# Attention, a gated layer and routed experts in one kernel: four routing tables, a moved sum and bound instruction orders

## The chip, the cores and the metric

The kernel is one program on 1 core of a Trainium2 chip. The metric is the device time of one execution in microseconds (us), shown as the median of several runs. Five engines take part: TensorE (PE) for matrix products, VectorE (DVE), ScalarE (ACT), GpSimd (POOL) and SyncE (SP), which here only issues DMAs and reads registers. POOL issues DMAs too, all the indirect ones among them.

## The reference, cut to what matters

```
attn = softmax(mask(q k^T / 8 + bias)) v        # 4 x 8 heads, 576 positions, 64 wide, window of 128
x    = attn as [2304, 512]
x    = (sigmoid(x w_gate) * (x w_val)) w_out    # [512, 1536] twice, [1536, 512]
logits = normalised(x) . normalised(expert_emb) / tau      # 8 experts
e      = argmax(logits)                                     # one expert for each token
out[t] = softmax(logits)[t, e] * (relu(x[t] w1[e]) w2[e])   # [512, 1024], [1024, 512]
```

All of it is in float32. The kernel makes each float32 product from three products of a high and a low part, so most operands are first split: ACT casts the high part and DVE subtracts it to get the low part.

## The kernel before, in words

The 2304 tokens are 18 tiles of 128. They are worked on in chunks of 2, 4, 4, 4 and 4 tiles. The gated layer takes chunks 1 to 4 in two groups of two (`PAIRS`), and each group uses a scheme of seven products in place of eight, for which sums of input halves (S1 to S4, built by `sum_x`) and of weight parts (T1 to T4, `sum_w`) are needed. `seven` lists the seven products m1 to m7 of one block f of 128 columns, with what evicts them: e1 copies bank a into the row c11, f6 into r1, e7 into c22, e4 into c21, and the products in bank a go on accumulating after each copy.

What the layer gives is kept for the product with w_out as sums too (`keep_g`): for two blocks f it forms four sums, S3, S2, S4 and S1, and stores each tile to DRAM. For the first group these sums are put off in a list, from which `catch_up` takes them later. Three of them are left when the second group's loop over f (12 blocks) begins.

Small tiles of [128, 513] come from the pool `mid`, which has ten of them (`row`). Operand tiles of 4 KB a partition come from a pool of 33 (`slot`).

The product with w_out runs over 14 steps (`SEQ`), each with two halves, and then once more for chunk 0 (`mm2`). Between these steps the table `AT2` places the routing of each finished block b of four tiles: `rx` turns its rows and takes their norm, `ra` (`route_a`) makes the logits and writes the rows with their gate weight to `x2_d` in DRAM, `route_b` counts each token's place among those of its expert with small products (`rk`), and scatters the token numbers into tables in DRAM (`tab_d`) with one indirect DMA for each tile. Blocks 3, 7 and 1 come first; then `close` fixes which experts start early and gathers three tiles of their tokens. The blocks of `LATE` are routed afterwards, their tokens placed behind these tiles (`bump`). Rows of x2 that are not yet there when the early gathers run are filled with zeros by `zero_rows`.

`places` reads token numbers from the tables: one DMA for each table and a `min`, since an empty place holds 2304. `gather` reads the rows. `by_count` orders the experts by their counts, and SP then reads that order into registers for the addresses of weight loads. The experts run in that order (`ffn1`, `ffn2`, or `tok_a` and `tok_b` for a single tile), with the weights of the next expert loaded and split meanwhile. At the end a loop over overflow tiles follows; its plan is the list of small DVE instructions from `pn` to `ov`, and its count `nov` is read by every engine.

The attention part and most of the first group are written out in program order. From the last nine products of the first group on, a planner orders each engine's instructions by its own cost estimates, with earlier program order first. `tc.keep_in_program_order(i)` binds an instruction behind the one traced before it on its engine, and `tc.issue_after(i)` binds what follows on that engine behind i; neither waits for i to finish. On each engine the order is then fixed, and an instruction that waits holds up those behind it.

Of the kernel before, what the change touches and what calls it, by code (L numbers as in the profile page):

```python
# [22 lines left out]
NT = B * S  # L23
# [18 lines left out]
LATE = (5, 6, 0)  # L42
# [3 lines left out]
NMID = 10  # L46
NWARM = 7
CHUNKS = [2, 4, 4, 4, 4]
PAIRS = [(2, 1), (4, 3)]
# [9 lines left out]
def attn_ffn_moe(ctx: ExitStack, tc: tile.TileContext, qkd, vd, wgv, w_out, emb, tau, w1, w2, cst, ids, out):  # L59
# [10 lines left out]
    tab_d = [dram.tile([P * E * TCOL, 1], I32, tag=f"tab_d{y}", name=f"tab_d{y}") for y in range(2)]  # L70
# [257 lines left out]
    def sum_x(key, x, y, op, q=nc.vector):  # L328
        t = slot([P, 2, 512], F32, f"xq_{key}")
        q.tensor_tensor(out=t, in0=x, in1=y, op=op)  # L330
        xf[key] = t

    def builds(pair):
        one, two = PAIRS[pair]

        def src(half, k):
# [6 lines left out]
            "S4+": lambda: sum_x((pair, "S4"), src(0, 1), xf[pair, "S2"], ALU.subtract, nc.gpsimd if pair else nc.vector),  # L343
# [102 lines left out]
    def catch_up(n=1):  # L446
        for t in [put_off.pop(0) for _ in range(min(n, len(put_off)))]:
            t()
# [4 lines left out]
    def keep_g(pair, f, half, gate, val, keep_val=True):  # L453
# [6 lines left out]
        def sums(name, t, x, y, op):  # L460
            def form():
                o = t()
                nc.vector.tensor_tensor(out=o, in0=K[x], in1=K[y], op=op)
# [414 lines left out]
    bB["S4+"]()  # L878
    WO_AT = [[], [0], [1], [2], [3], [4], [5, 6], [7], [8], [9], [10], []]
    for f in range(KF):  # L880
# [6 lines left out]
        if f == 0:  # L887
            bB["A22"]()
            bB["S4"]()
# [17 lines left out]
        if f < 3:  # L907
            catch_up()
# [38 lines left out]
    def places(o, x, c0, q):  # L947
        for t, v in zip((o, x), tab_v):
            q.dma_start(t, v[:, bass.ds(c0, o.shape[1])])
        nc.vector.tensor_tensor(out=o, in0=o, in1=x, op=ALU.min)  # L950


    def zero_rows():
        zrow = row("zrow")
        tc.keep_in_program_order(nc.gpsimd.memset(zrow, 0.0))
        nc.gpsimd.dma_start(x2_d[NT:NT + 1, :], zrow[0:1, :])
        for b in LATE:
            for u in range(2):
                nc.gpsimd.dma_start(x2_d[(2 * b + u) * P:(2 * b + u + 1) * P, :], zrow)
# [18 lines left out]
    cp.tile([P, 8], I32, tag="pad", name="pad")  # L978
    idx0, idx1 = (cp.tile([P, 2 * CE], I32, tag=f"idx{y}", name=f"idx{y}") for y in range(2))
    routed, mark, reg = {}, {}, {}  # L980
# [26 lines left out]
    def route_a(b, ss, xr, c=None):  # L1007
# [17 lines left out]
        nc.scalar.copy(parts, part[:, 0:nu * P])  # L1025
        lp = pt("s", f"lp{b}", 2)
# [32 lines left out]
    def route_b(b):  # L1059
# [41 lines left out]
    def by_count(c, less, o, n):  # L1101
# [539 lines left out]
```

## Time and profile before

| what | value |
|---|---|
| median of 3 runs | 819.44 us (818.62 to 820.49) |
| the profiled execution | 817.23 us |
| its span, first to last instruction | 815.6 us |
| mean granted clock of PE | 0.988 of full speed |
| PE busy | 782.7 us, 96% of the span |
| DVE, ACT, POOL busy | 72%, 56%, 27% |
| HBM traffic | 216 GB/s over the span |

The span is that of the profiled execution, and what lies around it is the rest of that execution's own time. PE's busy time counts pipelined products by modelled ends, so that busy isn't the same as at its peak. Where PE idles, the view of waits tells which instruction on which engine ended the idle time. A product of 512 columns starts 0.23 us after the one before it at full clock.

### The profile page before, as it was taken

How to read it: one execution, taken by the hardware profiler on the slowest of the kernel's cores; microseconds unless marked ns; L12 is line 12 of the kernel's file. 1: busy time of each engine (PE TensorE's matmuls, PEld its weight loads, DVE VectorE, ACT ScalarE, POOL GpSimd, SP SyncE). 2: the span in 40 equal slices, each digit the busy share in tenths (PEclk: the TensorE clock that was granted, in tenths of full speed). 3: DMA queues.
4: the chain of work that ended last, by engine and by line, in shares of the span. 5: the costliest groups of instructions: out<-in, count | busy, mean ns of one | idle time of the engine just before them, and what ended most of it. 6: DMA issues, size and time to landing. Idle time of an engine off the chain costs nothing. (4 is left out here: it accounts for less than half of the span.)

```text
span 815.6 us, 15736 instructions
## 1 busy us (share of the span) xinstructions
PE 782.7 (96%) x5585; PEld 654.1 (80%) x5585; DVE 585.7 (72%) x1361; ACT 452.7 (56%) x955; POOL 219.1 (27%) x343
## 2 busy tenths in 40 slices
PE   9989999999999899999999999979899999999996
PEld 6767888878887688887787777757679989899995
DVE  7988978888899978897867587717656564446621
ACT  6888766666545455556656667646345443354510
POOL 6856423322001022232100033534422120402100
PEclk9999999999999899999999999989999999999999
DMA  8686468765674698999875487673459555626100
GB/s 284 185 269 217 157 254 282 269 234 192 230 255 175 212 374 322 342 344 383 338 257 181 156 238 229 132 221 93 152 181 319 182 184 180 204 104 230 58 25 19
DMA packets 73761, 176.64 MB, mean 217 GB/s; under 512 B 10548, under 2 KB 18612, under 8 KB 73680
## 3 DMA queue, kind: packets, MB, share of 16 engines
q1 hardware_dynamic: 63248, 145.07, 51.9%
q0 software_dynamic: 10432, 30.53, 11.3%
q8 instruction: 45, 0.74, 0.4%
q14 instruction: 36, 0.29, 0.1%
HBM read 120.93 MB, written 55.35 MB: 216 GB/s over the span
## 5 line engine op out<-in xcount | busy, mean ns | idle before, releaser
L1175 PE MATMUL h<-xe,weh 128*128 128x256 f32 (+4 forms) x512 | 105.3, 299 | 0.1
L116 POOL TENSOR_SCALAR p<-p,rs 128x192 f32<-128x192 f32 x140 | 77.0, 569 | 91.3 <-DVE rs L267 54.5
L120 DVE TENSOR_TENSOR wel<-wer,weh 128x1024 fp32r<-128x1024 f32 x64 | 76.9, 1220 | 25.3 <-ACT weh L104 9.8
L1175 PEld LDWEIGHTS h<-xe,weh 128*128 128x128 f32 x512 | 83.2, 188 | 1.5 <-DVE h L1178 0.7
L251 ACT ACTIVATE p<-p,mx 128x192 f32<-128x192 f32 x144 | 64.1, 447 | 27.6 <-DVE mx L248 27.3
L1175 PE MATMUL h<-xe,wel 128*128 128x256 f32 (+4 forms) x256 | 76.2, 298 | 0.0
L104 ACT CAST weh<-wer 128x1024 fp32r<-128x1024 f32 x64 | 66.2, 1048 | 15.8 <-DMA wer<-in_w 10.6
L1193 PE MATMUL z<-weh,h 128*128 128x512 f32 (+1 forms) x224 | 72.0, 398 | 0.7 <-ACT h L1177 0.7
L1177 ACT ACTIVATE h<-h 128x256 fp32r<-128x256 f32 (+4 forms) x64 | 26.7, 418 | 76.8 <-PE h L1175 75.3
L1178 DVE SCALAR_TENSOR_TENSOR h<-h,h 128x256 fp32r<-128x256 f32 (+4 forms) x64 | 29.4, 463 | 39.4 <-ACT h L1177 39.0
L120 DVE TENSOR_TENSOR ol<-ol,oh 128x1024 fp32r<-128x1024 f32 x42 | 49.7, 1217 | 9.7 <-ACT oh L104 9.7
L1193 PEld LDWEIGHTS z<-weh,h 128*128 128x128 f32 (+1 forms) x224 | 40.8, 186 | 10.0 <-ACT h L1177 0.9
L1175 PEld LDWEIGHTS h<-xe,wel 128*128 128x128 f32 x256 | 48.3, 188 | 0.0
L1298 PE MATMUL b<-oh,wo 128*128 128x512 f32 x144 | 44.9, 393 | 0.0
L1193 PE MATMUL z<-wel,h 128*128 128x512 f32 (+1 forms) x112 | 44.2, 394 | 0.0
L1198 POOL DMA_INDIRECT out<-y,cols x13 | 14.3, 1101 | 102.3 <-DVE y L1197 97.8
L104 ACT CAST oh<-ol 128x1024 fp32r<-128x1024 f32 x42 | 41.4, 1048 | 0.0
L1197 DVE TENSOR_SCALAR y<-z,xg 128x512 f32<-128x512 f32 (+1 forms) x16 | 12.0, 748 | 37.6 <-PE z L1193 37.6
L1298 PE MATMUL b<-oh,th 128*128 128x512 f32 x96 | 38.1, 401 | 0.0
L1298 PE MATMUL b<-oh,tl 128*128 128x512 f32 x96 | 38.1, 397 | 0.0
L1298 PE MATMUL b<-ol,th 128*128 128x512 f32 x96 | 37.9, 395 | 0.0
L237 PE MATMUL s<-qk 64*64 64x128 f32 (+2 forms) x864 | 34.6, 278 | 1.6 <-DVE mx L248 0.7
(481 smaller groups left out, 2222.7 us busy)
## 6 DMA issues: line engine op xcount, KB each, us to landing
wer<-in_w SPq DMA_DIRECT2D x64, 512.0 KB, 5.2
wr<-in_wgv SPq DMA_DIRECT2D x24, 512.0 KB, 5.9
qk<-in_qkd SPq DMA_DIRECT2D x36, 320.0 KB, 3.9
v<-in_vd SPq DMA_DIRECT2D x36, 192.0 KB, 3.5
wor<-in_w_out SPq DMA_DIRECT2D x12, 512.0 KB, 6.3
ol<-g0S SPq DMA_DIRECT2D x12, 512.0 KB, 6.6
ol<-g1S SPq DMA_DIRECT2D x12, 512.0 KB, 5.0
wq_d<-wh SPq DMA_DIRECT2D x10, 512.0 KB, 2.8
```

Source lines behind the costliest of these rows:

```text
L104: nc.scalar.copy(o, i)
L116: nc.gpsimd.tensor_scalar(out=t, in0=t, scalar1=r, scalar2=0.0, op0=ALU.mult, op1=ALU.add)
L120: e.tensor_tensor(out=o, in0=i, in1=h.bitcast(F32), op=ALU.subtract)
L237: nc.tensor.matmul(ss[u][y * 64:(y + 1) * 64, j * WK + d:j * WK + d + n], q[halves[u], a:a + 64], k[halves[u], a + c0:a + c0 + n], start=T ...
L251: nc.scalar.activation(out=o, in_=o, func=AF.Exp, scale=-1.0, bias=mx[:, z:z + 1], accum_out=su[:, z:z + 1])
L1175: nc.tensor.matmul(m[:, :n], w[:, fs], x[:, k, :], start=(cnt == 0), stop=(cnt == 3 * KD - 1))
L1177: nc.scalar.activation(out=hh, in_=m[:, :n], func=AF.Relu)
L1178: nc.vector.scalar_tensor_tensor(out=hl, in0=m[:, :n], scalar=0.0, in1=hh.bitcast(F32), op0=ALU.max, op1=ALU.subtract)
L1193: nc.tensor.matmul(m[0:w, :], h, ww[:, ds], start=(cnt == 0), stop=(cnt == 3 * KE - 1))
L1197: nc.vector.tensor_scalar_mul(y[0:w, :], m[0:w, :], x[0:w, DM:DM + 1])
L1198: nc.gpsimd.indirect_dma_start(out=out, out_offset=IOA(ap=idx[0:w], axis=0), in_=y[0:w, :], in_offset=None, bounds_check=NT - 1, oob_is_er ...
L1298: nc.tensor.matmul(bk[pair, z], p, q, start=(first and kk == 0 and y == 0), stop=(kk == KF // 2 - 1 and y == 2), skip_group_check=True)
```

## The change

Six edits, most of them about the order of the work.

1. There are four routing tables instead of two, one for each tile of a block. `places` reads all four into one tile and takes the minimum in two steps, so it issues four DMAs where it issued two. The tables are cleared by four DMAs at the start.
2. The halves of the second group are exchanged, (3, 4) for (4, 3), and with them the blocks 5 and 7 in the order of routing. The block routed after `close` is then 7, with the highest token numbers, and the early gathers are bounded to the first 14 tiles. `zero_rows` clears the end row and the first two tiles, where it cleared six tiles, and is placed at step 5 of the second product in place of step 11. The memsets of the tiles for the early gathers are bound behind what was traced before them on POOL, and each expert's gathers follow its table reads.
3. The sum S4 of the second group is formed on DVE in place of POOL, and traced after A22 in block 0.
4. The three sums that are left of the first group are bound to the end of blocks 0, 1 and 2.
5. The register loads of the experts' order are bound behind the SP instructions traced before them, and the overflow plan behind what was traced last on each engine when expert 3 begins.
6. `route_a` can stop before the small product that folds the logits (`route_l`, which waits for `parts`); for blocks 7 and 0 that part comes one place later.

A padding tile grows from 8 to 16 columns, and the tiles `more` of the table reads become two that are used in turn, so that the tiles behind them keep their offsets modulo 128 bytes.

```diff
-LATE = (5, 6, 0)
+LATE = (7, 8, 0)
+NE = (LATE[0] - 1) * 2 + 2
+NTAB = 4
-PAIRS = [(2, 1), (4, 3)]
+PAIRS = [(2, 1), (3, 4)]
...
-            "S4+": lambda: sum_x((pair, "S4"), src(0, 1), xf[pair, "S2"], ALU.subtract, nc.gpsimd if pair else nc.vector),
+            "S4+": lambda: sum_x((pair, "S4"), src(0, 1), xf[pair, "S2"], ALU.subtract),
...
-    def catch_up(n=1):
+    def catch_up(n=1, pin=False):
         for t in [put_off.pop(0) for _ in range(min(n, len(put_off)))]:
-            t()
+            t(pin)
...
-            def form():
+            def form(pin=False):
                 o = t()
-                nc.vector.tensor_tensor(out=o, in0=K[x], in1=K[y], op=op)
+                i = nc.vector.tensor_tensor(out=o, in0=K[x], in1=K[y], op=op)
+                if pin:
+                    tc.keep_in_program_order(i)
...
     bB["S3"]()
-    bB["S4+"]()
...
             bB["A22"]()
+            bB["S4+"]()
             bB["S4"]()
...
         if f < 3:
-            catch_up()
+            catch_up(pin=True)
...
     def places(o, x, c0, q):
-        for t, v in zip((o, x), tab_v):
-            q.dma_start(t, v[:, bass.ds(c0, o.shape[1])])
-        nc.vector.tensor_tensor(out=o, in0=o, in1=x, op=ALU.min)
+        for y, v in enumerate(tab_v):
+            q.dma_start(x[:, y, :], v[:, bass.ds(c0, o.shape[1])])
+        nc.vector.tensor_tensor(out=x[:, 0:2, :], in0=x[:, 0:2, :], in1=x[:, 2:4, :], op=ALU.min)
+        nc.vector.tensor_tensor(out=o, in0=x[:, 0, :], in1=x[:, 1, :], op=ALU.min)
...
-        tc.keep_in_program_order(nc.gpsimd.memset(zrow, 0.0))
+        nc.gpsimd.memset(zrow, 0.0)
         nc.gpsimd.dma_start(x2_d[NT:NT + 1, :], zrow[0:1, :])
-        for b in LATE:
-            for u in range(2):
-                nc.gpsimd.dma_start(x2_d[(2 * b + u) * P:(2 * b + u + 1) * P, :], zrow)
+        for u in range(2):
+            nc.gpsimd.dma_start(x2_d[u * P:(u + 1) * P, :], zrow)
...
+        held[b] = ss, xr, lg, parts
+        if now:
+            route_l(b)
+
+    def route_l(b):
+        ss, xr, lg, parts = held.pop(b)
+        nu = len(xr)
...
-            nc.gpsimd.indirect_dma_start(out=tab_d[u % 2], out_offset=IOA(ap=ai[:, u:u + 1], axis=0),
+            nc.gpsimd.indirect_dma_start(out=tab_d[u], out_offset=IOA(ap=ai[:, u:u + 1], axis=0),
...
-        order.extend(nc.sync.value_load(ord_e[0:1, j:j + 1], min_val=0, max_val=E - 1) for j in range(o, o + n))
+        with tc.issue_after(latest(ENG.SP)[0]):
+            order.extend(nc.sync.value_load(ord_e[0:1, j:j + 1], min_val=0, max_val=E - 1) for j in range(o, o + n))
...
-            places(idx0[:, e * CE:e * CE + n], idx1[:, e * CE:e * CE + n], reg[e] * TCOL, nc.gpsimd)
-        for t in range(CE):
-            gather(0, t, idx0[:, t:t + 1], NT)
-        gather(1, 0, idx0[:, CE:CE + 1], NT)
+            places(idx0[:, e * CE:e * CE + n], idxs[e], reg[e] * TCOL, nc.gpsimd)
+            for t in range(n):
+                gather(e, t, idx0[:, e * CE + t:e * CE + t + 1], NE * P)
...
-            nc.gpsimd.memset(x, 0.0)
+            tc.keep_in_program_order(nc.gpsimd.memset(x, 0.0))
...
+        (5, 1, 0): [zero_rows],
-        (10, 0, 0): [lambda: rx(7, 0)], (10, 0, 1): [lambda: rx(7, 1), lambda: ra(7)], (11, 0, 0): [lambda: route_b(7), zero_rows],
+        (10, 0, 0): [lambda: rx(5, 0)], (10, 0, 1): [lambda: rx(5, 1), lambda: ra(5)], (11, 0, 0): [lambda: route_b(5)],
-        (14, 0, 0): [lambda: rx(5, 0), behind(1, lambda: we0(0))],
-        (14, 0, 1): [lambda: rx(5, 1), lambda: ra(5), behind(1, lambda: we0(1))],
-        (14, 1, 0): [lambda: route_b(5), lambda: we0(2)], (14, 1, 1): [early_x, lambda: we0(3)], (14, 1, 2): [lambda: we0(4)],
+        (14, 0, 0): [lambda: rx(7, 0), behind(1, lambda: we0(0))],
+        (14, 0, 1): [lambda: rx(7, 1), lambda: ra(7), behind(1, lambda: we0(1))],
+        (14, 1, 0): [lambda: rl(7), lambda: we0(2)], (14, 1, 1): [lambda: route_b(7), early_x, lambda: we0(3)],
+        (14, 1, 2): [lambda: we0(4)],
...
+        if e == 3:
+            marks = latest(ENG.PE, ENG.DVE, ENG.Activation, ENG.Pool, ENG.SP)
...
+    pinned = ExitStack()
+    for i in marks:
+        pinned.enter_context(tc.issue_after(i))
...
     nov = nc.values_load(ov[0:1, 2 * MAXOV:2 * MAXOV + 1], min_val=0, max_val=MAXOV)
+    pinned.close()
```

## Rows read from the trace of the kernel before

**Rows 1.** The page's first part: busy us of each engine, share, instructions.

```profile
PE 782.7 (96%) x5585; PEld 654.1 (80%) x5585; DVE 585.7 (72%) x1361; ACT 452.7 (56%) x955; POOL 219.1 (27%) x343
```

**Rows 2.** Windows of 20 us: busy us (instructions) of each engine, granted clock, DMA share, GB/s.

```profile
260.00:280.00 20.00, 15.64 (x59) 12.03 (x59) 18.87 (x26) 10.77 (x13) 2.68 (x1) 0.83 0.34 122
...
540.00:560.00 20.00, 18.23 (x96) 14.33 (x99) 10.54 (x49) 11.30 (x26) 10.43 (x13) 0.76 0.53 156
...
580.00:600.00 20.00, 15.78 (x76) 11.95 (x75) 15.42 (x52) 7.71 (x11) 5.00 (x4) 1.00 0.62 195
...
640.00:660.00 20.00, 20.00 (x112) 18.83 (x111) 11.79 (x17) 9.07 (x14) 0.00 (x0) 1.00 0.50 157
```

**Rows 3.** PE's waits over the span: us in total, times, longest us.

```profile
PE lp L1029 <- ACT parts L1025: 4.4, 2, 3.6
...
PE c L437 <- DVE c L566: 2.0, 1, 2.0
...
PE ht L1234 <- DVE wel L120: 1.6, 1, 1.6
...
PE a L437 <- ACT xh_(1, 'S3')_3995 L104: 1.6, 1, 1.6
...
PE ht L1234 <- ACT weh L104: 1.4, 1, 1.4
...
PE rk L1071 <- DVE oh L1055: 1.2, 2, 0.7
```

**Rows 4.** Timeline 261.5 to 266.3 us: start, us, engine, line, instruction, idle before.

```profile
262.07 2.68 POOL L330 TENSOR_TENSOR xq_(1, 'S4')_3999<-xf,xq_(1, 'S2')_3911 128x1024 f32<-128x1024 f32 x1 [60.39 <-DVE xq_(1, 'S2')_3911 L330]
...
262.09 0.42 DVE L384 TENSOR_TENSOR tf<-wt 128x256 f32<-128x256 f32 x1
...
262.43 2.60 DVE L386 TENSOR_TENSOR tf<-wt,tf 128x256 f32<-128x256 f32 x1
...
265.68 0.51 PE L437 MATMUL c<-xh_(0, 'S4')_2002,wh 128*128 128x512 f32 x1 [1.98 <-DVE c L566]
```

**Rows 5.** DVE's timeline at 274 us.

```profile
273.88 0.68 DVE L463 TENSOR_TENSOR c<-c,c 128x512 f32<-128x512 f32 x1
```

**Rows 6.** Timelines of DVE and of POOL, 496 to 517 us.

```profile
496.96 0.22 DVE L1037 TENSOR_SCALAR sb_x<-sb_x,itau 128x4 f32<-128x4 f32 x1
...
514.73 2.03 DVE L1037 TENSOR_SCALAR sb_x<-sb_x,itau 128x4 f32<-128x4 f32 x1
...
515.25 1.48 POOL L1138 MEMSET xg<- 128x513 f32 x3
```

**Rows 7.** POOL's timeline, 526 to 546 us.

```profile
526.11 1.42 POOL L1090 DMA_INDIRECT tab_d<-ids_sb,ai  x1 [1.80 <-DMA tab_d<-ids_sb,ai]
...
530.03 1.22 POOL L1090 DMA_INDIRECT tab_d<-ids_sb,ai  x1 [0.30 <-issue]
...
542.05 1.14 POOL L949 DMA_DIRECT2D idx<-tab_d  x2 [9.67 <-DMA tab_d<-ids_sb,ai]
...
545.04 1.06 POOL L1139 DMA_INDIRECT xg<-x_d,idx  x1 [1.85 <-DVE idx L950]
```

**Rows 8.** PE's timeline at the first transpose of the gathered rows.

```profile
548.63 0.30 PE L1155 MATMUL tx<-cs,xg 128*128 128x128 f32 x1 [1.07 <-DMA xg<-x_d,idx]
```

**Rows 9.** ACT's timeline at 538 us.

```profile
538.53 0.59 ACT L1025 COPY parts<-part 128x512 f32<-128x512 f32 x1 [2.19 <-DMA x_d<-xr]
```

**Rows 10.** DMA issues, 519 to 545 us: count, KB each, median us to landing.

```profile
x_d<-xr POOLq DMA_DIRECT2D x4, 256.5 KB, 10.7
...
idx<-tab_d POOLq DMA_DIRECT2D x2, 0.5 KB, 6.9
```

**Rows 11.** Waits of SP's queue, 486 to 620 us.

```profile
SPq L1113 <- DVE pn L1533: 31.7, 1, 31.7
```

**Rows 12.** DVE's groups by line, 577 to 591 us: count, busy us, mean ns.

```profile
L1552 DVE SCALAR_TENSOR_TENSOR el<-le,pe,el 1x16 f32<-1x16 f32 x7 | 1.6, 226 | 0.1
```

**Rows 13.** DMA issues, 284 to 310 us.

```profile
g1A<-c POOLq DMA_DIRECT2D x2, 256.0 KB, 5.8
```

More of the change, by code (lines that the diff above doesn't have):

```diff
@@ L69, in attn_ffn_moe @@
     x2_d = dram.tile([NT + 1, DM + 1], F32, tag="x2_d", name="x2_d")
-    tab_d = [dram.tile([P * E * TCOL, 1], I32, tag=f"tab_d{y}", name=f"tab_d{y}") for y in range(2)]
+    tab_d = [dram.tile([P * E * TCOL, 1], I32, tag=f"tab_d{y}", name=f"tab_d{y}") for y in range(NTAB)]
     wf_d = dram.tile([KF * P, 2 * KD * P], F32, tag="wf_d", name="wf_d")
@@ L326, in split_x, with sum_x @@
             lo_sub("v", xs[key][1], src, xs[key][0])
-    def sum_x(key, x, y, op, q=nc.vector):
+    def sum_x(key, x, y, op):
         t = slot([P, 2, 512], F32, f"xq_{key}")
-        q.tensor_tensor(out=t, in0=x, in1=y, op=op)
+        nc.vector.tensor_tensor(out=t, in0=x, in1=y, op=op)
         xf[key] = t
@@ L977, in attn_ffn_moe @@
     nc.vector.memset(bump, 0.0)
-    cp.tile([P, 8], I32, tag="pad", name="pad")
-    idx0, idx1 = (cp.tile([P, 2 * CE], I32, tag=f"idx{y}", name=f"idx{y}") for y in range(2))
-    routed, mark, reg = {}, {}, {}
+    cp.tile([P, 16], I32, tag="pad", name="pad")
+    idx0 = cp.tile([P, 2 * CE], I32, tag="idx0", name="idx0")
+    idxs = [cp.tile([P, NTAB, n], I32, tag=f"idxs{e}", name=f"idxs{e}") for e, n in enumerate(EARLY)]
+    routed, mark, reg, held = {}, {}, {}, {}
     def few(n, tag, name, *shape, dt=F32):
@@ L1005, in route_xs, with route_a @@
         return ss, xr, c
-    def route_a(b, ss, xr, c=None):
+    def route_a(b, ss, xr, c=None, now=True):
         nu = len(xr)
@@ L1339, in rx, with rl @@
     def rx(b, z):
-        pair, row_ = {1: (0, 2), 3: (0, 1), 5: (1, 2), 7: (1, 1)}[b]
+        pair, row_ = {1: (0, 2), 3: (0, 1), 5: (1, 1), 7: (1, 2)}[b]
         xs2[b] = route_xs(b, [cq[pair, f"{row_}1"], cq[pair, f"{row_}2"]], (2 * z, 2 * z + 1), xs2.get(b))
     def ra(b):
-        route_a(b, *xs2.pop(b))
+        route_a(b, *xs2.pop(b), now=b not in LATE)
+    def rl(b):
+        route_l(b)
     def we0(j):
@@ L1413, in weights @@
             split_we(e, j, load_we(order[e], j, e), "a", "v")
-    hs = ffn1(0, CE * P, between={0: [lambda: route_a(0, *late)], 1: [lambda: we0(5)], 2: [lambda: we0(6)], 4: [lambda: we0(7)]})
+    hs = ffn1(0, CE * P, between={0: [lambda: route_a(0, *late, now=False)], 1: [lambda: route_l(0), lambda: we0(5)], 2: [lambda: we0(6)], 4: [lambda: we0(7)]})
     route_b(0)
@@ L1427, in load_col @@
         cols[e] = cp.tile([P, nt], I32, tag=f"cols{e}", name=f"cols{e}")
-        other = cp.tile([P, nt], I32, tag=f"more{e}", name=f"more{e}")
+        other = cp.tile([P, NTAB, 3], I32, tag=f"more{e % 2}", name=f"more{e}")[:, :, 0:nt]
         places(cols[e], other, reg.get(e, order[e]) * TCOL + t0, nc.gpsimd if e in reg else nc.sync)
@@ L1564, in attn_ffn_moe @@
         ix = sm.tile([P, 1], I32, tag="ovix", name="ovix")
-        places(ix, sm.tile([P, 1], I32, tag="ovjx", name="ovjx"), cv, nc.sync)
+        places(ix, sm.tile([P, NTAB, 1], I32, tag="ovjx", name="ovjx"), cv, nc.sync)
         X = E
```

## The prediction

> **What bounds the kernel now.** I read the page's busy times first. TensorE (PE) is busy 782.7 us of the 815.6 us span [rows 1], so what a change is worth is what it does to PE's other 33 us and to the matmuls that run at the lower clock. The windows of 20 us come next: from 600 us to the tail PE is never idle for long (640 to 660 us stands for ten such rows), and 300 to 380 us is full as well; the loss lies in three stretches, 260 to 280, 520 to 560 and 580 to 600 us, and in the first two the granted clock also falls, to 0.83 and 0.76 of full speed [rows 2]. PE's waits then give names [rows 3], and the timelines of the other engines say why each producer was late. Everything before 260 us, 280 to 510 us and the expert loop after 600 us is bound by PE itself, so an edit there is worth nothing unless it makes a new wait.
>
> **Stretch one, 260 to 290 us.** POOL's sum S4 for the second group (2.68 us from 262.07) lies across DVE's L386, a 128x256 subtraction that takes 2.60 us there, while its twin L384 takes 0.42 [rows 4]. DVE is late by 2.18 us, its addition for c22 too, and PE waits 1.98 us [rows 3, 4]. Behind the wait the clock falls: a mean of 0.83 over 20 us is 3.4 us withheld (part of the time at 1.2 GHz instead of 2.4), half of it here and half behind the next wait, so some 1.6 us [rows 2]. The change gives S4's sum to DVE, behind A22, so the collision goes. Not all of 1.98 + 1.6 is kept, because the next thing that PE needs, the hi part of S3, comes through the same full DVE and a cast on ACT, and PE waits 1.6 us for it already [rows 3]. That point moves with DVE: by 2.18 us, and by about 0.6 us more, since DVE itself waited some 0.6 us for PE just before S3. I take 2.8. In exchange DVE gets a 128x1024 sum (its like take 1.22) ahead of S4's split, and loses three put-off sums of 0.68 us, the first at 273.88 [rows 5]; the balance is between -0.5 and +0.6 us, and I take nothing.
>
> The three put-off sums are bound behind the end of blocks f = 0, 1 and 2. Their DVE time lies in the gaps that DVE has in each block, waiting for ACT's copies. What is not free is memory: the first group's last six rows (of ten in the pool `mid`) stay in use up to 30 us longer, and their stores join a queue that is full at 284 to 304 us. No row of before shows such a wait; the bound is 0 below and some 4 us above (one late landing of 5.8 us [rows 13], less the 1.4 us of matmuls that PE has between a copy and the next use of the bank). I take 0.5, since the planner knows the pool's size. Stretch one: 2.8 - 0.5 = 2.3, between -1.7 and 3.4.
>
> **Stretch two, 510 to 556 us.** Here is the routing of the second-to-last block and of the last large one. The losses: 0.69 us for `oh` and 3.61 us for `parts` [rows 3], 1.07 us for the gathered rows at 548.63 [rows 8], 0.5 us for the next `oh` (the rest of the 1.2 in that row), and the clock. A mean of 0.76 over 20 us withholds 4.8 us; some of that fell on idle time, so 4.5. Sum 0.7 + 3.6 + 1.1 + 0.5 + 4.5 = 10.4 us.
>
> What feeds these waits: (a) three memsets of gather tiles run early on POOL at 515.25, and DVE's tiny L1037 takes 2.03 us beside them, against 0.22 in the block before [rows 6]. The change binds each memset behind the table reads; `oh`, the count and the scatters come about 1.8 us earlier, and the 0.69 goes. (b) The three tiles taken so early also occupy rows; ACT's copy of `parts` waits 2.19 us for a row whose store has not landed [rows 9]. With those rows free, six zero writes fewer in the queue, and `lp` traced behind twelve matmuls (2.8 us of cover), I expect the 3.61 to go; if a row is still late, 3.61 - 2.8 = 0.8 stays. (c) The third scatter waits 1.80 us for the first, which shares its table; the fourth is issued behind the four row stores, and the reads of its table wait until 542.05, 12 us after its issue at 530.03 [rows 7]. The gather follows at 545.04 and PE has its rows 3.6 us later [rows 7, 8].
>
> With four tables no scatter waits for another. The price is four reads instead of two in each place: two more issues of 0.55 us on POOL (three places before the experts' loop) and two on SP later, where the queue has time between its loads, and a second `min` of 0.16. Between 574 and 578 us POOL's extra 2.2 us delay gathers that PE needs only at 594, so they are covered; without that cover they cost 2.2.
>
> How early is the first transpose? If PE never stalled it would come at 548.63 - 1.07 - 0.69 - 3.61 - about 3.1 of slow matmuls = 540.1. The chain: the first scatter at 521.26 - 1.8 = 519.5, four scatters of 1.0 to 1.75 us with gaps of 0.3 to 525, the four stores 2.2 us, the reads issued by 528.7, landing 6.9 us later [rows 10], gather, 3.6 us: about 540. If the planner keeps a scatter behind the stores, as now, its landing still takes up to 12 us, and the chain ends at 548.63 - 1.8 - 1.8 + the two reads added (1.1) = 546.2. So the gain is between 2.4 and 10.4. The stores land 10.7 us after issue now [rows 10]; they will start some 3.6 us sooner, partly before SP's weight loads, which puts the likeliest chain at 543 to 544 and a wait of 3 to 4 us with a little of the slow clock. I take 6.0.
>
> The Trainium skill (DMA: Bandwidth & Descriptors, Anatomy of one DMA — SWDGE (gpsimd) path) gives a transfer from GpSimd's queue 2.0 us plus its bytes over 436 GB/s; for a 256.5 KB store that is an estimate of 2.6 us. The trace does not agree here: 10.7 us [rows 10]. By the rule a scatter would land in some 2 us even behind the stores, nothing would be left of stretch two's wait, and the total would be that of the second rival.
>
> The exchange of the halves only renames: rows (1,1) and (1,2) of the output are finished at the same steps as before, and the last block now has the highest tokens, so the early gathers are bounded instead of zero-filled. Two more table clears at 15 us are two SP issues of 0.47 us; five units of q and k are loaded ahead, so they are covered, and cost 1 us at most without it. The new offsets cost nothing that the rows could show: equal casts and subtractions stay within 2% of one another wherever their tiles lie.
>
> **Stretch three, 556 to 600 us.** SP sits 31.7 us in the loads of the experts' order [rows 11]; the last five weight tiles of expert 1 are queued behind it and are issued from 581.47. The change puts those register loads behind them. By my count of the 33 slots (16 with expert 0's halves, nine with expert 1's first three tiles, two with x) six are free from about 560, so the tiles land before PE needs them. DVE also runs 49 small instructions of the overflow plan between 578 and 590.6, one group of them 7 times 226 ns [rows 12]; they are bound behind the start of expert 3, where DVE is half idle. PE's 1.6 us for `wel` and 1.4 for `weh` [rows 3] fall away, and 0.76 of `lp` for the last small block, which now has matmuls ahead of it: 3.8 us. The 1.2 us for the transposed hidden rows stays. PE comes here earlier and DVE has the same halves to subtract, so I take 3.3, between 1.5 and 4.2.
>
> **Sum.** 2.3 + 6.0 + 3.3 = 11.6 us. The profiled execution took 817.23 us, 1.63 outside the span; it would take 805.6. The median of the runs is 819.44, 2.2 above it, so the forecast is 819.44 - 11.6 = 807.8. About 0.2%, 1.6 us, is what a measurement of this kernel can tell.
>
> **Rivals.** *The chain stays behind the stores:* the last scatter or the reads queue behind 1 MB of rows as now; 2.3 + 2.4 + 3.3 = 8.0, 811.4. For it: the planner already placed stores between scatters. Against: the wait that put the fourth scatter last is gone. *Nothing is left:* the queue is empty enough, 2.8 + 10.4 + 4.2 = 17.4, 802.0; the skill's rule says this, the landing of 10.7 speaks against it. *Slower:* rows. If in blocks 0 to 2 ACT's copy out of PE's bank waits 5 us for a store to land, PE waits each time: 819.44 - 12.1 + 15 = 822.3. It decides from 4.0 us a block. For it: six of ten rows are held, and the block itself wants five; against: DVE can form the sums as soon as they are allowed. *The waits return elsewhere:* DVE becomes late for `wel`, or the bound memsets sit before the gathers, and what is won at 540 is lost by 600; 816 to 820.
>
> **Numbers.** Forecast 0.47 (own range 804.5 to 811), chain behind stores 0.22, nothing left 0.13, slower 0.07, returned 0.11 (0.03 of it faster, 0.06 the same, 0.02 slower). Faster 0.85, same 0.06, slower 0.09. The range reaches from 801 to 816.5 and leaves out the slower rival and part of the last.
>
> **What would show it.** Right: L386 back at 0.42 and no PE wait for c22; L1037 near 0.22; PE's wait for `parts` under 1 us and a clock of 0.9 or more at 530 to 550; no SP wait of 31 us, expert 1's tiles issued before PE reaches them. Wrong: ACT waiting for the first group's stores at 275 to 300 us; table reads still waiting ten microseconds; PE waiting at S3 longer than 1.6 us because S4's sum slipped ahead of it.

## The result, and the profile after

The changed kernel takes 822.87 us (median of 20 runs), the kernel before 817.39 us (20 runs beside them): ratio 1.0066, 95% interval 1.0051 to 1.0081. It is slower by 0.66%, some 5.5 us, where 11.6 us less were forecast (from 819.44, the median of three runs; over 20 runs the kernel before is 2 us lower). The profiled execution of the changed kernel took 825.32 us with a span of 823.6, 8.0 us more than the one of before.

PE's part of the first part of the page, beside [rows 1]: 3.9 us more busy for the same 5585 matmuls, which is more of them at the lower clock (a mean of 0.975 against 0.988), and 37.0 us not busy where before had 32.9.

```profile
PE 786.6 (96%) x5585; PEld 657.7 (80%) x5585; DVE 583.2 (71%) x1372; ACT 449.1 (55%) x953; POOL 216.9 (26%) x346
```

The windows of 20 us of the changed kernel, with the columns of [rows 2]:

```profile
260.00:280.00 20.00, 17.45 (x73) 13.86 (x72) 17.73 (x24) 9.87 (x13) 0.00 (x0) 0.85 0.54 190
...
300.00:320.00 20.00, 17.93 (x73) 14.73 (x74) 14.75 (x23) 11.38 (x18) 2.81 (x6) 0.91 0.94 345
...
540.00:560.00 20.00, 12.15 (x54) 9.51 (x53) 6.52 (x29) 8.36 (x18) 5.29 (x7) 0.66 0.57 122
...
580.00:600.00 20.00, 13.62 (x54) 10.33 (x52) 4.79 (x9) 2.05 (x4) 9.80 (x13) 0.83 0.30 82
...
640.00:660.00 20.00, 20.00 (x111) 19.07 (x111) 14.01 (x19) 10.43 (x16) 3.19 (x3) 1.00 0.72 220
```

260 to 280 us has improved by 1.8 us of busy PE. A new loss has come at 300 to 320 us, where PE had been full at full clock; 540 to 560 us is 6 us idler than before and its mean clock is down from 0.76 to 0.66; 580 to 600 us is 2 us idler and now has a clock of 0.83. PE's waits over the whole span name the three new losses:

```profile
PE tx L1167 <- DMA xg<-x_d,idx: 6.1, 2, 5.1
PE ht L1246 <- DVE wel L122: 5.4, 1, 5.4
PE a L439 <- ACT r L562: 4.3, 4, 2.8
...
PE a L439 <- ACT xh_(1, 'S3')_3997 L106: 1.8, 1, 1.8
PE lp L1041 <- ACT parts L1030: 1.7, 1, 1.7
```

The wait for `c` is gone, and `parts` and `oh` have shrunk, as foreseen [rows 3]. The others are in new places.

Two marks on PE divide the span: the first transpose for a routing (tile `tc`), at 434.34 us before and 437.64 after, and the first matmul with 384 tokens (expert 2), at 636.71 and 644.16. So 3.3 us are lost ahead of the first mark, 4.2 between the marks and 0.5 behind. Of the 3.3, 1.4 are lost by 257 us, with a clock of 0.85 at 60 to 80 us. That much is within what executions differ by: at the same matmul the profiled executions of the kernels below lie between 254.6 and 257.4 us, and four that have before's program up to there between 255.0 and 256.4.

**At 300 us.** ACT's timeline, and PE's first matmul behind it, each with the idle time ahead of it:

```profile
300.88 0.66 ACT L126 ACTIVATE cvwo<-wor 128x512 f32<-128x512 f32 x1 [5.88 <-issue]
301.45 0.57 ACT L562 COPY r<-a 128x512 f32<-128x512 f32 x1
```

```profile
302.07 0.79 PE L439 MATMUL a<-xh_(1, 'S3')_3997,wh 128*128 128x512 f32 x1 [2.78 <-ACT r L562]
```

The conversion `cvwo` waits 5.88 us, for something that the view can't name; the copy that PE needs is queued behind it. In the same stretch SP's queue has a long wait, for the sum that a put-off store is to write (before has at most 1.3 us for that):

```profile
SPq L460 <- DVE c L465: 14.8, 1, 14.8
```

**At 520 to 554 us.** POOL's timeline:

```profile
523.13 1.74 POOL L1102 DMA_INDIRECT tab_d<-ids_sb,ai  x1 [10.16 <-DVE ai L1095]
...
529.74 1.23 POOL L1102 DMA_INDIRECT tab_d<-ids_sb,ai  x1 [0.30 <-issue]
530.97 0.59 POOL L953 DMA_DIRECT2D idxs<-tab_d  x1
531.55 2.17 POOL L1063 DMA_DIRECT2D x_d<-xr  x4
533.71 1.09 POOL L953 DMA_DIRECT2D idxs<-tab_d  x2
535.99 0.54 POOL L953 DMA_DIRECT2D idxs<-tab_d  x1 [1.19 <-DMA tab_d<-ids_sb,ai]
...
542.43 0.54 POOL L953 DMA_DIRECT2D idxs<-tab_d  x1 [2.75 <-DMA x_d<-xr]
547.16 1.07 POOL L1151 DMA_INDIRECT xg<-x_d,idx  x1 [4.18 <-DVE idx L955]
```

No scatter waits for another, as the four tables promised; but the four row stores stand ahead of seven of the eight reads, as in the kernel before they stood ahead of all four [rows 7]. The DMA issues of 519 to 546 us (last column: median us from issue to landing):

```profile
x_d<-xr POOLq DMA_DIRECT2D x4, 256.5 KB, 10.6
...
idxs<-tab_d POOLq DMA_DIRECT2D x4, 1.0 KB, 10.6
```

The medians hide what a store ahead costs a read. Here is what the view of the reads' line gives, before (519 to 546 us) and after (the four reads of 1 KB, 530.9 to 536.4 us):

```profile
DMA to landing us min/median/max: 1.9/6.9/10.7
```

```profile
DMA to landing us min/median/max: 6.0/10.6/11.7
```

Taken one by one, the two reads of before that follow the stores at once took 10.7 and 10.3 us, and the two of 542 us, when the stores had landed, 1.9 and 3.4. In the changed kernel the read issued ahead of the stores took 6.0, the three of 1 KB behind them 11.7, 11.4 and 9.8.

PE is ready earlier than before and waits for the gathered rows, [rows 8] against:

```profile
551.00 1.08 PE L1167 MATMUL tx<-cs,xg 128*128 128x128 f32 x4 [5.14 <-DMA xg<-x_d,idx]
```

**At 580 to 591 us.** DVE's timeline, and PE's:

```profile
587.70 0.16 DVE L954 TENSOR_TENSOR more<-more 128x2 int32<-128x2 int32 x1 [6.82 <-DMA more<-tab_d]
...
589.36 0.17 DVE L954 TENSOR_TENSOR more<-more 128x4 int32<-128x4 int32 x1 [1.31 <-DMA more<-tab_d]
...
589.64 2.38 DVE L122 TENSOR_TENSOR wel<-wer,weh 128x1024 fp32r<-128x1024 f32 x2
```

```profile
590.93 1.22 PE L1246 MATMUL ht<-wel,xe 128*128 128x512 f32 x2 [5.41 <-DVE wel L122]
```

DVE takes its instructions in order. A `min` over the places of expert 0 waits 6.82 us for the reads of its tables, and two lo halves of expert 1's weights, which PE waits for, are queued behind it.

### The profile page after: what moved, and what is told of

Its sections match the earlier page's. It is cut to its first block, busy times and chain, and to the rows that moved or that the text cites. A ratio compares the mean times of both kernels' runs of the same rounds, so it can differ in the third digit from the quotient of the medians.

```text
span 823.6 us, 15796 instructions
## 1 busy us (share of the span) xinstructions
PE 786.6 (96%) x5585; PEld 657.7 (80%) x5585; DVE 583.2 (71%) x1372; ACT 449.1 (55%) x953; POOL 216.9 (26%) x346
## 5 line engine op out<-in xcount | busy, mean ns | idle before, releaser
L1210 POOL DMA_INDIRECT out<-y,cols x13 | 12.9, 993 | 101.5 <-DVE y L1209 62.4
```

The costliest lines, as they stand in the source:

```text
L1210: nc.gpsimd.indirect_dma_start(out=out, out_offset=IOA(ap=idx[0:w], axis=0), in_=y[0:w, :], in_offset=None, bounds_check=NT - 1, oob_is_er ...
```

## The experiments

All are timed in five rounds beside the kernel before, but for the one without row stores (three). Marks and the first transpose of gathered rows (`tx`) are those of each kernel's profiled execution; such a figure can be off by a us or two, like the 1.4 us above, so the ratio decides.

| kernel | ratio to before, 95% | mark 1 | first `tx` | mark 2 |
|---|---|---|---|---|
| before | 1 | 434.3 | 548.6 | 636.7 |
| changed | 1.0066 (1.0051 to 1.0081) | 437.6 | 551.0 | 644.2 |
| a1 sums free | 1.0002 (0.9984 to 1.0019) | 433.6 | 547.0 | 639.5 |
| a4 sums' stores on POOL | 1.0071 (1.0045 to 1.0096) | 435.5 | 548.2 | 642.5 |
| a9 sums behind block 0 | 1.0027 (1.0011 to 1.0044) | 433.0 | 545.7 | 636.2 |
| b5 before + new start | 0.9986 (0.9963 to 1.0008) | 434.0 | 546.2 | 632.1 |
| a2 two tables | 1.0083 (1.0057 to 1.0109) | 436.7 | 552.1 | 643.5 |
| a7 row stores by ACT | 1.0006 (0.9985 to 1.0027) | 435.4 | 543.5 | 634.3 |
| a10 no row stores | 0.9991 (0.9970 to 1.0012) | 437.5 | 544.2 | 632.9 |
| b4 before + row stores by ACT | 0.9981 (0.9960 to 1.0001) | 434.7 | 543.8 | 635.2 |
| a5 routing in one | 1.0058 (1.0035 to 1.0081) | 437.1 | 549.7 | 640.2 |
| a6 mins behind 6th half | 1.0070 (1.0047 to 1.0093) | 436.3 | 549.4 | 641.5 |
| b2 before + order loads, plan | 1.0019 (0.9999 to 1.0039) | 435.3 | 548.0 | 633.4 |
| b6 b2 + mins behind 4th half | 0.9952 (0.9934 to 0.9970) | 434.3 | 547.8 | 629.7 |
| c1 a7 + a9 | 0.9955 (0.9934 to 0.9977) | 433.2 | 541.5 | 631.7 |
| c2 c1 + two tables | 0.9942 (0.9921 to 0.9963) | 435.2 | 543.5 | 632.3 |
| c4 c1 + routing in one | 0.9978 (0.9964 to 0.9992) | 433.8 | 541.2 | 635.1 |
| c5 c1 + mins behind 4th half | 0.9964 (0.9943 to 0.9984) | 433.7 | 541.5 | 630.4 |
| d1 b5 + b4 + b6 | 0.9918 (0.9888 to 0.9948) | 435.6 | 545.6 | 632.5 |
| d2 c2 + mins behind 4th half | 0.9932 (0.9906 to 0.9957) | 433.7 | 544.5 | 630.2 |

### The put-off sums: rows of the pool or SP's queue?

My first theory was SP's wait of 14.8 us, with weight loads behind it; the rival was the prediction's own, the rows of the pool. Sums free (a1):

```
-            catch_up(pin=True)
+            catch_up()
```

> The changed kernel, in which the three put-off sums of blocks f = 0 to 2 are again free to be placed by the planner; all else as changed. Theory Q (SP's queue): in the changed kernel the store of a bound sum stands 14.8 us at the head of SP's queue, the weight loads behind it leave 10 us late, ACT waits for one of them until 300.9 us and PE loses 2.8 us and then some 2 us to the lower clock. Then SP's wait of 14.8 us goes, PE has no wait at 300 us, and the time is 4 to 5 us under the changed kernel's 822.9: 818 to 819, about level with before. Theory R (rows of the pool stay occupied): the same time; it is told apart by the next kernel. Rival E (the loss lies elsewhere, in the later stretches alone): 822 to 823.

816.64 us: the whole loss comes back, and PE's wait at 300 us is gone. The gain at the start shrinks as well: the first matmul on S3's hi part comes at 273.17 us, 2.6 earlier than before, but the first on S4's at 284.56 against 285.07: DVE has the put-off sums and S4's sum to do before it.

The sums bound, their stores alone moved to POOL's queue (a4):

```
-        def put(name, t):
-            (nc.gpsimd if pair else nc.sync).dma_start(...)
+        def put(name, t, late=False):
+            (nc.gpsimd if pair or late else nc.sync).dma_start(...)
...
-                put(name, o)
+                put(name, o, pin)
```

> The changed kernel with the sums still bound behind blocks 0 to 2, their stores alone issued from POOL's queue and no longer from SP's. The rows stay occupied as long as in the changed kernel. Theory Q (SP's queue): SP's wait of 14.8 us goes, the weight loads leave by 283 us, PE does not wait at 300 us, 818 to 819. Theory R (rows): ACT still waits near 300 us for as long as 5.9 us, and the time stays at 822 to 823.

821.85 us. SP's wait of 14.8 us is gone and its weight loads leave by 284 us, but ACT's timeline has the wait still:

```profile
299.03 0.66 ACT L126 ACTIVATE cvwo<-wor 128x512 f32<-128x512 f32 x1 [5.47 <-issue]
```

So SP's queue was not what this wait hangs on. The programs as built, with the semaphores that each instruction waits for, say what was (the changed kernel, a4 and a1):

```
L126 ACTIVATE cvwo0_4161<-wor0_3975 128x512 [waits DMAHW4_49,DMASW2_49,DVE_49]
L126 ACTIVATE cvwo0_4161<-wor0_3975 128x512 [waits DMAHW4_49,DMASW3_49,DVE_49]
L126 ACTIVATE cvwo0_4161<-wor0_3975 128x512 [waits DMAHW1_49]
```

The DMAHW is the load of `wor`, which left at 266.40 us. The DMASW is a store from POOL's queue: six of the pool's ten rows are held by the sums, the remaining ones come round within one block, and `cvwo` gets the row of a tile whose store has just been issued. In the changed kernel that store leaves POOL at 295.51 us and lands 5.3 us later, at 300.81, and `cvwo` starts at 300.88. In a4 it leaves at 293.12; the one landing of its kind that the trace has took 5.5 us, which gives an estimate of 298.6, and `cvwo` starts at 299.03.

All three sums bound behind block 0, so that the rows come free before block 1's stores (a9):

```
-        if f < 3:
-            catch_up(pin=True)
+        if f == 0:
+            catch_up(3, pin=True)
```

> The changed kernel with all three put-off sums bound behind the end of block f = 0, in place of one behind each of the blocks 0, 1 and 2; all else as changed. Theory R (six rows of the pool of ten stay occupied until the sums' stores have landed, so that ACT's conversion at 300 us gets a row whose store has just been issued): the rows are free by 295 us, ACT no longer waits 5.9 us at 300 us, PE not 2.8 us, and the S4 operands are still 2 to 4 us earlier than in the kernel with free sums; the mark at 434 us comes 2 to 4 us earlier than in the changed kernel, 818 to 820. Rival D (three sums of 0.7 us and three stores crowd one gap of DVE): PE waits for DVE at 288 to 295 us for 2 us or more, 821 to 823.

817.52 us, and `cvwo` no longer waits on a store of POOL's:

```profile
292.18 0.66 ACT L126 ACTIVATE cvwo<-wor 128x512 f32<-128x512 f32 x1
```

The rows theory holds for that wait. What is left at 300 to 320 us is another: ACT's cast of `wt` waits for its load and not for a row, and PE's copy is queued behind it.

```profile
306.50 1.04 ACT L106 CAST wh<-wt 128x1024 fp32r<-128x1024 f32 x1 [3.42 <-DMA wt<-tf_d]
307.45 0.58 ACT L562 COPY r<-a 128x512 f32<-128x512 f32 x1
```

```profile
308.08 0.50 PE L439 MATMUL a<-xh_(1, 'S3')_3997,wh 128*128 128x512 f32 x1 [1.27 <-ACT r L562]
```

That load leaves SP at 293.26 us and lands 13.2 us later. SP's queue has waited 12.9 us for a bound sum ahead of it, and ten weight loads then leave within 7 us. So the first theory has a part in what remains.

The start alone on the kernel before (b5: S4's sum on DVE behind A22, the three sums bound behind block 0):

> The kernel before with the change at the start of the second group alone: S4's sum on DVE behind A22, and the three put-off sums bound, all behind block f = 0 (where the rows come free in time). Theory of the prediction, mended by the rows: POOL's collision and PE's wait for c22 go, and the mark at 434 us comes 1.5 to 2.5 us earlier than in before; ratio 0.997 to 0.998. Rival (DVE is full from 260 to 285 us, so that what S4's sum takes there is lost again at the next operand): the mark within 0.5 us of before's, ratio 0.9995 to 1.0005.

814.77 us, ratio 0.9986 with an interval that reaches 1.0008: perhaps 1 us, not told from none. PE is busy 17.05 us of 260 to 280 at clock 1.00, where before had 15.64 at 0.83 [rows 2]; some of it goes back at 300 to 320 us (18.69 us busy), with the same wait behind `wt` as in a9. The mark is 0.3 us earlier, which by itself is the rival. But from the matmul at 257 us to the mark the eight kernels with this start take 178.0 us in the mean (177.0 to 179.6), four with the start of before 179.0 (178.9 to 179.4): about 1 us again.

### The table reads: four tables, and what stands ahead of them

Two tables in the changed kernel (a2: `NTAB = 2`, one `min`, scatters to `tab_d[u % NTAB]`):

> The changed kernel with two routing tables instead of four: two reads and one min at each place, two scatters to each table. All else as changed. Theory T (the reads of four tables, through POOL's queue, make DVE's min late by 6.8 us, and the lo halves of expert 1 queue behind it): PE's wait of 5.4 us for wel falls under 2 us, and the first gathered rows come some 1 to 2 us earlier; 817 to 820. Theory L (the min is late because the last small block's routing was cut in two and its scatters come 5 us later): PE's wait for wel stays at 3 us or more, 821 to 824. If two tables bring back the third scatter's wait for the first, the first transpose comes 2 us later and the time goes up by as much.

824.13 us, not told from the changed kernel. PE's wait for `wel` falls from 5.4 to 3.4 us, that for gathered rows rises from 6.1 to 10.8. The wait for `wel` stays above the 2 us of theory T, and the first `tx` comes 2 us later against the mark, as expected if the third scatter waits again; four tables are no gain and no loss that shows.

The four row stores of the second-to-last block from ACT's queue (a7):

```
-            nc.gpsimd.dma_start(x2_d[t0:t0 + P, :], xr[u])
+            (nc.scalar if b == 1 else nc.gpsimd).dma_start(x2_d[t0:t0 + P, :], xr[u])
```

> The changed kernel with the four row stores (256.5 KB each) of the second-to-last block issued from ACT's queue and no longer from POOL's; all else as changed. Theory S (the table reads stand behind these stores in POOL's queue): the reads land within 3 to 5 us of their issue, the first transpose of gathered rows comes by 546 us, PE's wait of 6.1 us falls under 1.5, and 4 to 5 us come back: 817.5 to 819. Rival B (the weight loads of 2 MB that leave SP's queue at 530 us, and the stores wherever they are issued, fill the memory's path): the reads still take 8 to 10 us, the wait stays above 4 us, 821 to 824.

816.07 us: 0.60% comes back, nearly all of the loss and more than expected. The DMA issues of 519 to 546 us:

```profile
x_d<-xr ACTq DMA_DIRECT2D x4, 256.5 KB, 4.7
...
idxs<-tab_d POOLq DMA_DIRECT2D x4, 1.0 KB, 5.7
idxs<-tab_d POOLq DMA_DIRECT2D x4, 0.5 KB, 2.5
```

From the first mark to the first `tx` it takes 108.1 us, 113.4 in the changed kernel. PE's wait for gathered rows did not fall under 1.5 us, it is 6.3, since PE is there sooner too; its wait for `wel` falls from 5.4 to 2.2. But here the stores also leave 8 us earlier (523.1), ahead of the weight loads. So the stores were left out (a10, zeros in their rows 100 us earlier), which keeps the weight loads where they were:

> The changed kernel without the four row stores of the second-to-last block (their rows of x_d are filled with zeros some 100 us earlier, so that part of the result is left out); all else as changed. Queue theory: with no stores ahead of them the table reads land 2 to 4 us after issue, as in the kernel with the stores in ACT's queue, and the first transpose comes 5 to 7 us earlier against the mark at 434 us than the changed kernel's 113.4 us. Memory theory: the 2 MB of weights that SP loads at 530 us are as much in the way as the stores; the reads still take 7 us or more and the first transpose comes less than 3 us earlier.

```profile
idxs<-tab_d POOLq DMA_DIRECT2D x4, 1.0 KB, 4.0
```

106.7 us from mark to `tx`, 6.7 less, with six weight loads of 512 KB issued in the same stretch. The 4.0 is the median of two landings, all that the trace has of the four: 5.7 us for the third read and 2.4 for the fourth, issued 4 us later. So it is the stores in POOL's queue that make the reads late; the weight loads alone leave them at 5.7. That it is the order in the queue, and not the stores' bytes, this run can't say, since the bytes are gone too. The changed kernel's trace speaks for the order: the reads issued from 533.71 to 538.22 us all landed within 0.8 us behind the last store (545.25), however early they left.

The kernel before, with the row stores by ACT alone (b4):

> The kernel before with one edit alone: the four row stores of the second-to-last block issued from ACT's queue. If the table reads' place behind these stores is what sets the chain before as well, the reads of 542.05 us come 6 to 9 us earlier and the first transpose with them; PE's 1.1 us for the gathered rows goes, but its 3.6 us for parts stays, since that hangs on a row of the pool: 1 to 3 us faster, ratio 0.996 to 0.999. Rival (before, PE reaches that point too late for the chain to matter): 1.000.

815.46 us, 0.9981: within what was expected, but with an interval that reaches 1.0001, not told from none. The waits went the other way than expected: PE's 3.6 us for `parts` fell to 0.8, and that for gathered rows rose to 5.4, since PE is there sooner.

### Expert 1's weights: SP, or a min in DVE's order?

The kernel before with the order loads and the overflow plan moved (b2):

> The kernel before with two parts of the change alone: the register loads of the experts' order stand behind the weight loads in SP's queue, and the overflow plan is bound behind the start of expert 3. Theory of the prediction: SP's wait of 31.7 us goes, expert 1's weights come in time, PE's 1.6 us for wel and 1.4 for weh go: 3 us faster than before, ratio 0.996 to 0.997. Rival G (something else, the places or the gathered rows, is late next at 580 to 600 us): ratio 0.999 to 1.001, with a new wait there of 2 us or more.

817.04 us: nothing gained, the rival. SP's wait of 31.7 us [rows 11] is gone, and the weights come in time, as ACT's timeline shows: both casts are done by 574.6 us. DVE's:

```profile
572.59 1.99 ACT L104 CAST weh<-wer 128x1024 fp32r<-128x1024 f32 x2
```

```profile
577.66 0.16 DVE L950 TENSOR_TENSOR cols<-cols,more 128x1 int32<-128x1 int32 x1 [3.87 <-DMA more<-tab_d]
...
580.37 2.35 DVE L120 TENSOR_TENSOR wel<-wer,weh 128x1024 fp32r<-128x1024 f32 x2
```

```profile
581.64 0.74 PE L1235 MATMUL ht<-wel,xe 128*128 128x512 f32 x2 [3.02 <-DVE wel L120]
```

The same order as in the changed kernel: a `min` that waits for reads, and ready halves behind it. That `min` bound behind the fourth lo half, on top of b2 (b6):

```
+        with tc.issue_after(after) if after else nullcontext():
             nc.vector.tensor_tensor(out=o, in0=o, in1=x, op=ALU.min)
...
-        places(cols[e], other, ..., nc.gpsimd if e in reg else nc.sync)
+        places(cols[e], other, ..., nc.gpsimd if e in reg else nc.sync,
+               wel_at[1, 3] if e < 2 else None)
```

> The kernel before with the order loads and the overflow plan moved as in the change (which alone measured 1.0019), and the mins over the places of experts 0 and 1 bound on DVE behind the fourth lo half of expert 1. Theory M (DVE's order: a min that waits 3.9 us stands ahead of two lo halves that are ready): PE's wait of 3.0 us for wel falls under 1 us, and 2 to 3 us come back, ratio 0.998 to 0.9995. Rival G (the gathered rows come later by what the halves come earlier): a new wait of PE for gathered rows at 585 to 600 us, ratio 1.001 to 1.003.

```profile
576.60 2.35 DVE L120 TENSOR_TENSOR wel<-wer,weh 128x1024 fp32r<-128x1024 f32 x2
578.87 0.23 DVE L951 TENSOR_TENSOR cols<-cols,more 128x1 int32<-128x1 int32 x2
```

812.57 us, 0.9952, more than expected: PE no longer waits for `wel`, and the mins, which by then have their reads, lose nothing. Of the 0.67% to b2 (5.5 us) the two profiles show 2.7 us between the marks; the rest is within the two intervals. In the changed kernel the mins were bound behind the sixth half (a6):

> The changed kernel, with the two mins over the tables' reads for experts 0 and 1 (before the experts' loop) bound on DVE behind the sixth lo half of expert 1's weights. Theory M (DVE works in order, and the min that waits 6.8 us for its reads holds up two lo halves that are ready): PE's wait of 5.4 us for wel goes, and with it most of the lower clock at 580 to 600 us; 5 to 6 us under the changed kernel, 817 to 818. Rival G (the gathers that need the mins come later and PE waits for them instead): 821 to 824, with PE waiting for gathered rows near 600 us.

822.41 us: the rival. The sixth half waits for its own weights, the gathers come late behind it, and PE waits for them in place of `wel`:

```profile
PE tx L1168 <- DMA xg<-x_d,cols: 4.8, 2, 2.9
```

The routing of the last two blocks in one piece again, in the changed kernel (a5):

> The changed kernel with the routing of the last large and the last small block in one piece again, placed as before the change; the four tables, the bound sums and the rest stay. Theory L (the small block's logits are held for a step, its scatters come 5 us later than before, and the reads of the places with them): the scatters of that block come 4 to 5 us earlier, DVE's wait of 6.8 us for the reads and PE's 5.4 us for wel shrink to under 2 us, and 3 to 4 us come back: 818 to 820. Rival T (the reads of four tables are slow by themselves): PE's wait for wel stays above 4 us, 821 to 824. In both, the waits for parts may come back with up to 3 us before 565 us.

821.38 us: not told from the changed kernel, and PE's wait for `wel` stays at 4.2 us. The cut does not explain it.

### Together

Both mended parts on the changed kernel (c1 = a7 + a9), and three kernels made from it:

> The changed kernel with two edits together: the four row stores of the second-to-last block issued from ACT's queue, and all three put-off sums bound behind block f = 0. If the two losses are separate, as theory says (rows of the pool at 300 us; table reads behind the row stores at 530 us), their gains add: ratios of 0.994 and 0.996 against the changed kernel's 1.0066 give 0.996 to 0.998 against before, 813 to 815. Rival (what one gives back the other already had, because a later wait takes it): 1.000 to 1.002.

> The kernel with both edits (row stores from ACT, sums behind block 0), and two routing tables in place of four. Theory: with the stores out of POOL's queue a scatter lands soon, so that sharing a table costs one wait of some 2 us for the third scatter, and the four reads fewer give 2.2 us of POOL's time and an earlier min at 585 us back: within 2 us of the same kernel with four tables. Rival: four tables are what makes the first transpose early; without them it comes 4 us later, and the time goes up by 3 us or more.

> The kernel with both edits (row stores from ACT, sums behind block 0), and the routing of the last large and of the last small block in one piece as before the change. Theory L (holding the logits back makes the last small block's table entries and the min over them late): PE's wait for wel at 580 to 590 us shrinks to under 1 us and 1 to 2 us come back against the kernel with both edits. Rival (the hold covers the copy of parts, which costs PE 2 to 3 us without it): 1 to 3 us slower than that kernel.

> The kernel with both edits (row stores from ACT, sums behind block 0; 0.9955 against before), and the mins over the places of experts 0 and 1 bound on DVE behind the fourth lo half of expert 1. Theory M: PE's wait of 2.1 us for wel goes and 1 to 2 us come back, ratio 0.993 to 0.994. Rival G: the gathered rows are late instead, 0.995 to 0.997.

813.70, 813.42, 816.00 and 813.34 us. The two gains add: 1.0066 becomes 0.9955. The row stores give back 0.60% and the sums 0.39% (0.64% where they are free, a1), together more than the loss of 0.66%; but the stores stood ahead of the reads before the change too, where moving them is worth 0.19% (b4), so not all of the 0.60% was lost by the change. Two tables can't be told from four; the cut routing seems worth some 2 us here (c4 against c1, intervals that overlap); the bound mins take PE's wait for `wel` away (c5) and give nothing that can be told. Last, the three mended losses on the kernel before (d1), and on the changed kernel with two tables (d2):

> The kernel before with S4's sum on DVE and the put-off sums bound behind block 0 (0.9986 alone), the row stores of the second-to-last block from ACT's queue (0.9981 alone), and the order loads, the overflow plan and the mins moved (0.9952 alone). If the three losses are separate, the ratios multiply: 0.992, that is 810 to 811. Rival (the earlier chain meets the later one, and one of them hides the other): 0.994 to 0.996.

> The changed kernel with row stores from ACT, sums behind block 0 and two tables (0.9942), and the mins bound behind the fourth lo half: 0.993 to 0.995, since with four tables that bound gave nothing that could be told (0.9964 against 0.9955). If the exchange of the halves, the bound memsets and the routing cut in two are worth something, it is faster than the first kernel of this call; if they cost, slower.

811.49 us (0.9918) and 811.93 (0.9932). The ratios of d1's parts multiply as expected. The two can't be told apart; by their ratios they are 5.6 to 6.7 us faster than the kernel before, and 11 to 12 faster than the changed one.

## Why the prediction was wrong

**Stretch one.** L386 (L388 in the changed kernel) takes 0.42 us, the wait for `c` went, and S3's hi part is used 2.2 us earlier (273.56 against 275.77) in an execution that was 1.4 us late on arrival: the 2.8 was of the right size there. The step that failed is "I take 0.5, since the planner knows the pool's size". What came was the bound above, a late landing: 2.78 us of PE's wait and the lower clock behind it, in one place. By a1 the binding costs 1.0066 - 1.0002, some 5 us. It was the rival *Slower*, by its mechanism, though with one such wait and not three; it had 0.07, although it counted that six of ten rows are held and the block wants five, which is the count that decided it. That its 822.3 us lies beside the measured 822.87 is luck: it kept the gains of the other two stretches and took three waits of 5 us.

**Stretch two.** Right: the memsets no longer collide (L1049 0.23 us, [rows 6]), `oh` waits 0.2 us, `parts` 1.7 and no scatter waits. Wrong: the chain. From the first scatter to the first `tx` it took 27.9 us, against 27.4 before [rows 7, 8]; by the forecast's own figures, 519.5 to 543 or 544, it should have been about 24. The first scatter came as forecast (523.13, or 519.8 without the 3.3 us lost ahead of the first mark). The step that failed is "landing 6.9 us later [rows 10]". The forecast puts the reads right behind the four stores, but the 6.9 is the median of two reads of 0.5 KB, one behind the stores (10.3 us) and one when they had landed (3.4). The reads of 1 KB behind the stores took 9.8 to 11.7 us. On top of that the last of the four left 4 us later than the 528.7 forecast (535.99, less the 3.3), since the scatters took 2.3 us longer and it waited 1.19 us for the last of them to land. Together these are 6.9 us, about what was forecast as gain; against the mark, the first `tx` came 0.9 us earlier than before. It is the rival *The chain stays behind the stores*, which named the reads, but left them 2.4 us of gain. And since PE came to the wait earlier, more of the wait was idle time, at a mean clock of 0.66.

The Trainium skill (DMA: Bandwidth & Descriptors, Queues, rings and completion order) says that each DMA engine goes round between the queues that it has work for, and, of the queues of SP and ACT, that their descriptors are consumed in ring order. The trace shows the like for POOL's queue: the reads behind 1 MB of stores all landed just behind the last of these stores. The turns between queues no run here shows by itself. The 2.0 us that the Trainium skill (DMA: Bandwidth & Descriptors, Anatomy of one DMA — SWDGE (gpsimd) path) gives, the ground of *Nothing is left*, shows where the queue had nothing ahead: the read of 542.05 us in the kernel before landed in 1.9 us.

**Stretch three.** That "the tiles land before PE needs them" was right, and worth nothing (b2). The step that failed is that PE's 1.6 and 1.4 us "fall away" with SP's late loads: just behind these stood a `min` in DVE's order, and without SP's wait PE waits 3.0 us for `wel` (b2). The forecast also covered the two reads added in each place because they "delay gathers that PE needs only at 594": what they delay first is the `min` that takes them in, and the weights' halves stand behind it on DVE. PE's wait there rose to 5.4 us in the changed kernel (3.4 with two tables, a2), and from the first `tx` to the second mark 5.1 us are lost against before. On the kernel before, with the `min` bound, the 3.3 us are there (b6: 0.48%, 3.9 us). In the changed kernel what the `min` costs is not shown: behind the sixth half the gathers come late (a6), and with the row stores by ACT the bound `min` gives nothing (c5).

**Sum.** The terms of 2.3, 6.0 and 3.3 us failed separately, by the runs above, each by work that stands in order ahead of what PE needs and waits for a transfer: a row of the pool, a DMA queue, a vector engine's queue.

**Still open.** That the start by itself gains (b5) shows in the marks, by about 1 us, and not in the times. The order in POOL's queue was not tried with the same stores leaving at the same time from another queue. The exchange of the halves and the bound memsets were not run alone; d2 and d1, which differ by them, the cut routing and little else, can't be told apart.

## What to carry to other kernels

When a change binds or adds a small instruction, ask what its tile keeps occupied and what stands behind it in its own engine and in its DMA queue; a min of 0.16 us or a store of 0.3 us costs as much as the transfer it waits for. A median over two transfers can stand for neither; look at each one with what was ahead of it in its queue. A wait that one engine shows last can hide another just behind it, so cover is to be checked for the second in line too. Parts that a change bundles are worth timing one by one: here one binding cost 0.64%, and the mended parts are worth 0.8% on the old kernel.

## What the runs showed of the hardware

Reads of 1 KB behind four stores of 256.5 KB in POOL's queue took 9.8 to 11.7 us to land, and all landed within 0.8 us behind the last store; without the stores one took 5.7 and one 2.4, though weight loads of 512 KB were under way in both; when the stores had landed, 1.9. The same stores landed in 4.7 us from ACT's queue and in 10.6 from POOL's; how much of that is because they left 8 us earlier is not shown. A tile whose store was just issued kept its row of the pool occupied until the store landed, 5.3 us, and ACT's next writer of that row waited for it. PE's wait of 5.14 us at 551 us goes with a clock of 0.66 over 20 us, so that a wait costs more than its length.
